# A three-part fp32 kernel: the first attention pair prepared in written order, smaller weight steps, a spread last pair, and a block diagonal copied from SBUF

## The chip, the cores and the metric

One core of a Trainium2 chip. TensorE (PE) multiplies, VectorE (DVE) and ScalarE (ACT) read its results from PSUM, GpSimd (POOL) adds from SBUF to SBUF, SyncE (SP) issues DMAs. The metric is the device time of one execution in microseconds.

## The reference, cut to what matters

```python
# q, k, v: 4 x 8 heads x 1152 x 64;  then x is 4 x 576 x 512
q_pool = q.reshape(B, H, S // 2, 2, D).mean(axis=3)
scores = scale * q_pool @ k.T;  scores -= scores.max(-1)
attn = exp(scores) / (exp(scores).sum(-1) + 1e-9);  x = attn @ v      # stage 1
# stage 2: 4 experts (two of them weighted in per token by a gate), causal attention 576 x 576
q, k, v = x @ wq[e], x @ wk[e], x @ wv[e];  out += gate * softmax(causal(q @ k.T)) @ v @ wo[e]
# stage 3: low-rank token mixing and an MLP 512 -> 2048 -> 512
u = x + (x.T @ U @ V).T;  out = u + relu(u @ w_ch1) @ w_ch2
```

U, V and the MLP's weights come as float64 and are decoded to float32 by integer operations on DVE.

## The kernel before

**Precision.** An fp32 operand of a product is cut into a high part (ACT copies it to fp32r) and a low part (DVE subtracts): `cut`, `evac_k`, `evac_q`. A score product is two matmuls with 128 contraction rows that carry high and low parts: tiles S1, S2 (from k) and Q1, Q2 (from q), held by `Pair`.

**Stage 1** works on 16 pairs of heads. A pair has 18 units (2 halves of 288 queries by 9 key blocks), and a unit has two slots (its two heads), so a pair is 36 slots. In a slot PE makes one score tile (L576, L577) and ACT its Exp (L578). After every third unit come the matmuls with v (L596). POOL adds up the denominators (L588). At the end of a half the sums, reciprocals and products follow (`post_a`, `post_r`, `post_b`; L428 to L441, L613).

**`prep(i)`** prepares pair i while pair i - 1 runs. `pool_q` adds neighbouring queries on DVE (L495). `tr_q` and `tr_k` transpose (L511, L502), ACT copies the high part (qh, kn), and one slot later DVE subtracts the low part (ql, klo). `tr_q` also sends qh by DMA into a block diagonal BD (L522). `lay` copies qh, ql, kn and klo by 12 DMAs into Q1, Q2, S1 and S2: six of 144 KB, six of 288 KB. `mxs` takes the maxima: one matmul of BD with 384 keys (L543), one reduce on DVE (L545), 27 per pair. `fin` turns the maxima of 5 or 4 query blocks by a transpose (L406), ACT copies them (`nm`, L408), and two DMAs put them as a row into Q2 (L411). L577 reads that row, so no score of a half starts before its `fin`. PSUM: `pms` has 3 buffers for maxima, transposes and sums.

**Order.** The steps stand in `side`, a list by slot; M_AT, Q_AT and the like are the slots. PE, DVE and ACT issue the loop over the slots (`attend`) in the order written (a manual region). What is emitted outside it, the whole preparation of pair 0 (all 27 maxima) and the first four steps of pair 1, and everything on SP, is ordered by the framework's planner. All DMAs are issued by SP, on one queue.

**Experts' weights** (`expert_weights`) are loaded and cut during stage 1 in six sets: wq, wk, wv with the gate, wo, U, V. A set has two 512-column cuts (wq to wo), or three decode steps of two DVE operations each and an end (U, V). The steps stand in slots 17 and 29 of a pair (WC_AT), a set every two pairs.

**Last pair.** In its slots the first expert pair is prepared: four cuts of x (XC_AT), four projections of 12 matmuls each (L684), maxima (L753) and `dmax`, which writes the maxima into Q2 on DVE (L395). `evac_q` takes a projection of q out of PSUM: two ACT copies to Q1 (L379); one slot later, for each half of the partitions, a DVE subtraction (L383), a DMA (L384) and an ACT copy of the same PSUM tile into the block diagonal (L385).

Of the kernel before, what the change touches and what calls it, by code (L numbers as in the profile page):

```python
# [27 lines left out]
WL_AT, WC_AT = 31, [17, 29]  # L28

XC_AT = [12, 13, 14, 15]  # L30
XP_AT = [18, 19, 21, 22, 25, 26, 27, 28, 29, 30, 31, 32, 33, 34, 35]
# [101 lines left out]
def kernel(  # L133
# [99 lines left out]

    def decode_steps(raw, a, b):
# [5 lines left out]
        def first():  # L240
            nc.vector.tensor_scalar(a, hi, 0x7FFFFFFF, None, op0=ALU.bitwise_and)
            nc.vector.tensor_scalar(f(a), f(a), F64_LEAST, F64_MOST, op0=ALU.max, op1=ALU.min)  # L242

        def second():
            nc.vector.tensor_scalar(a, a, 3, -0x40000000, op0=ALU.logical_shift_left, op1=ALU.bitwise_xor)  # L245
            nc.vector.tensor_scalar(b, lo, 29, None, op0=ALU.logical_shift_right)

        def third():
            nc.vector.scalar_tensor_tensor(b, a, 0x7FFFFFFF, b, op0=ALU.bitwise_and, op1=ALU.bitwise_or)
            nc.vector.scalar_tensor_tensor(b, hi, -0x80000000, b, op0=ALU.bitwise_and, op1=ALU.bitwise_or)  # L250

        return [first, second, third], f(b)

    def decode(raw, a, b):
        steps, v_ = decode_steps(raw, a, b)
        for g in steps:
            g()
        return v_

    def expert_weights():  # L260
# [16 lines left out]
        def heads(x, w, dst):  # L277
            t = part(x, NC, dst[0].shape[-1])

            def load():  # L280
                for e in range(E):
                    nc.sync.dma_start(t[:, :, e * HD:(e + 1) * HD], w[e].rearrange("(c p) d -> p c d", p=P))
                if t.shape[-1] > EW:
                    nc.sync.dma_start(t[:, :, EW:], w_gate.rearrange("(c p) e -> p c e", p=P))

            return load, pieces(t, *dst, 2)

        def out_():
            t = part(1, EP, DM)
            return (lambda: nc.sync.dma_start(t, wo.rearrange("(x e) d n -> (e d) x n", x=EP)) and None,  # L290
                    pieces(t, WO[0], WO[1], 2))
# [4 lines left out]
        def tokens_u():  # L296
            t = part(0, NTT, R, 2).bitcast(I32) if wide else part(0, NTT, R)
            steps, v_ = decode_steps(t, *(part(0, NTT, R, off=x * NTT * R).bitcast(I32) for x in (2, 3))) \
                if wide else ([], t)

            def load():
                nc.vector.memset(t[64:, full:], 0)
                m = mu.bitcast(I32) if wide else mu
                if wide:
                    nc.sync.dma_start(t[:, :full], m[:full * P].rearrange("(c p) (r w) -> p c r w", p=P, w=2))
                    nc.sync.dma_start(t[:T - full * P, full], m[full * P:].rearrange("p (r w) -> p r w", w=2))
                else:
                    nc.sync.dma_start(t[:, :full], m[:full * P].rearrange("(c p) r -> p c r", p=P))
                    nc.sync.dma_start(t[:T - full * P, full], m[full * P:])

            def end():
                cut(v_, MU[:, :, :R], MU[:, :, R:2 * R])
                nc.vector.memset(f(MU[:, :, 2 * R:3 * R]), 0.0)
                nc.scalar.activation(MU[:, :, 3 * R:], v_, AF.Copy)

            return load, steps + [end]

        def tokens_v():
# [16 lines left out]
        return [heads(0, wq, (WQK[0][:, 0], WQK[1][:, 0])), heads(1, wk, (WQK[0][:, 1], WQK[1][:, 1])),  # L335
                heads(0, wv, WVG), out_(), tokens_u(), tokens_v()]
# [39 lines left out]
    def evac_q(ps, bd, pr, sl, done):  # L376
# [36 lines left out]

    def run_all(steps):
        def run(g):
            x = g()
            for y in x if isinstance(x, tuple) else (x,):
                if callable(y):
                    run(y)

        for _, g in steps:
            run(g)
# [43 lines left out]
    def load_q(i):  # L466
        b, h0 = divmod(2 * i, H)
        qr = ld.tile([96, 2, JQ, 2, D], F32, name="qr")
        nc.sync.dma_start(qr, q[b, h0:h0 + 2].rearrange("h (p j u) d -> p h j u d", j=JQ, u=2))
        qraw[i] = qr  # L470

    def load_k(i):
# [3 lines left out]
        for j in range(0, NKT, w):  # L476
            for a in range(2):
                nc.sync.dma_start(kr[:, j:j + w, a, :],
# [3 lines left out]
    def load_v(i):  # L482
        b, h0 = divmod(2 * i, H)
        vr = per.tile([P, 2, NKT, D], F32, name="vr", bufs=2)
        nc.sync.dma_start(vr, v[b, h0:h0 + 2].rearrange("h (p j) d -> p h j d", j=NKT))
        vraw[i] = vr

    def prep(i):
# [18 lines left out]
        def tr_q(j0, j1):  # L507
# [9 lines left out]
            nc.scalar.activation(qh[:, sl], ps[:, :n], AF.Copy)  # L517

            def rest():
                nc.vector.tensor_sub(ql[:, sl], ps[:, :n], f(qh[:, sl]))  # L520
                for a in range(2):
                    nc.sync.dma_start(f(BD[i % 2][HALF[a], sl.start // 64:sl.stop // 64, HALF[a]]),  # L522
                                      f(qh[HALF[a], sl]).rearrange("p (t j) -> p t j", j=64))
# [32 lines left out]
        steps = [(POOL_AT, pool_q), (Q_AT[0], lambda: tr_q(0, 4)), (Q_AT[1], lambda: tr_q(4, JQ))]  # L556
        steps += [(at, lambda c=c: tr_k(c)) for c, at in enumerate(K_AT)]
        steps += [(LAY_AT, lay)] + [(at, lambda x=x: mxs(*x)) for at, x in zip(M_AT, order)]
        return steps + [(at, lambda x=x: fin(*x)) for at, x in zip(F_AT, BLOCKS)]
# [59 lines left out]
    P0, P1 = (sorted(prep(x), key=lambda y: y[0]) for x in range(2))  # L619
    turns = Q_AT + K_AT + [POOL_AT]  # L620
    load_q(0)
    load_k(0)
    run_all([x for x in P0 if x[0] in turns])
    load_k(1)
    load_q(1)
    load_v(0)
    run_all([x for x in P0 if x[0] not in turns and x[0] < F_AT[1]])
    run_all([x for x in P1 if x[0] < 0])
    run_all([x for x in P0 if x[0] == F_AT[1]])
    for x, (load, steps) in enumerate(expert_weights()):  # L630
        place(side, [(WL_AT, load)], n * 2 * x)
        at = [y + n * w for w in range(1, 3) for y in WC_AT]
        place(side, list(zip(at, steps)), n * 2 * x)
        assert len(steps) <= len(at)
    for i in range(NP):
        units += [unit(i, u) for u in range(2 * NKT)]
    for i in range(1, NP):
# [4 lines left out]
        place(side, [x for x in (P1 if i == 1 else prep(i)) if n0 + x[0] >= 0], n0)  # L642
# [268 lines left out]
    with tc.manual_schedule(engines={mybir.EngineType.PE, mybir.EngineType.DVE, mybir.EngineType.Activation}):  # L911
        attend(units, side)
# [186 lines left out]
```

## Time and profile before

| | |
|---|---|
| runs before, median (lowest to highest) | 1169.14 us (1166.94 to 1174.28), 3 runs |
| profiled execution: time, span | 1167.44 us, 1165.7 us |
| PE, DVE, ACT, POOL busy | 96%, 66%, 40%, 42% |
| granted TensorE clock, mean | 0.989 |
| DMA | 120.02 MB, one queue for all but instruction loads |

The span runs from the first to the last instruction; 1.7 us of the execution lie around it. Stage 1 takes the span from its start to about 500 us, stage 2 to about 760, stage 3 the rest. Matmuls are pipelined and their ends modelled, so PE's busy share hides short waits; the length of a repeated piece of work shows them.

### The profile page before, as it was taken

Reading aid. Unit: us, or ns where it says so; the run is one execution under the profiler, and the core shown is the slowest. Engines: PE = TensorE matmul, PEld = TensorE weight load, DVE = VectorE, ACT = ScalarE, POOL = GpSimd, SP = SyncE. Lnnn points to the kernel's source line nnn. Section 1 sums busy time; section 2 is a strip of 40 time slices with the busy share of each in tenths; the row PEclk is TensorE's granted clock in tenths of the full one; section 3 lists DMA queues with packets and bytes.
Section 4 is the critical chain, followed back from the end, with each engine's and each line's share of the span. In section 5 each row is a group of like instructions: output and inputs, shape, how many; then the busy total and the mean of one; then the engine's idle time right before and its main releaser. Section 6 shows DMA issues by size and latency. Waiting matters only on the chain.

```text
span 1165.7 us, 18965 instructions
## 1 busy us (share of the span) xinstructions
PE 1119.7 (96%) x6748; PEld 900.2 (77%) x6748; DVE 771.3 (66%) x1661; ACT 469.7 (40%) x1184; POOL 490.0 (42%) x382
## 2 busy tenths in 40 slices
PE   5999999999999999899999998999999999999998
PEld 3777777777777677678777775698979988999997
DVE  6687878787888877476858589989394256221222
ACT  1565656565555555544545545422221111111111
POOL 4688888888777788642212133212020011000000
PEclk7999999999999999999999999999999999999999
DMA  9787787878777664112112134363031011000111
GB/s 221 171 183 174 170 184 164 185 165 169 169 173 164 159 145 115 41 32 52 42 41 83 31 97 171 100 220 110 1 108 37 1 37 37 1 1 1 55 55 54
DMA packets 116957, 120.02 MB, mean 103 GB/s; under 512 B 71680, under 2 KB 88064, under 8 KB 116864
## 3 DMA queue, kind: packets, MB, share of 16 engines
q1 hardware_dynamic: 116864, 118.82, 41.3%
q8 instruction: 53, 0.87, 0.3%
q14 instruction: 40, 0.33, 0.1%
HBM read 52.65 MB, written 9.44 MB: 53 GB/s over the span
## 4 chain that ended last, share of the span: by engine, by line
PE 65%; DVE 17%; issue 11%; DMA 3%; ACT 2%; POOL 1%; SPq 1%; ACTq 0%; DVEq 0%; POOLq 0%
PE pv L596 10%; PE ms L1005 10%; PE o L1016 9%; PE ms L684 7%; PE st L576 7%; PE ms L543 5%; PE st L577 5%; PE pv L832 2%; DVE mp L545 2%; DVE dcb L250 1%; DVE dca L242 1%; PE ms L502 1%; DVE dca L245 1%; PE ms L603 1%; PE st L807 1%
## 5 line engine op out<-in xcount | busy, mean ns | idle before, releaser
L588 POOL TENSOR_TENSOR acc<-acc,pt 128x576 f32<-128x576 f32 x224 | 328.6, 1467 | 73.4 <-ACT pt L578 57.5
L578 ACT ACTIVATE pt<-st 128x288 f32<-128x288 f32 x576 | 218.8, 409 | 182.9 <-PE st L577 143.8
L545 DVE TENSOR_REDUCE mp<-ms 128x1 f32<-128x384 f32 x432 | 212.5, 545 | 55.0 <-PE ms L543 55.0
L1005 PE MATMUL ms<-uh,w 128*128 128x384 f32 x768 | 214.5, 340 | 0.0
L1009 DVE SCALAR_TENSOR_TENSOR hl<-ms,hh 128x384 fp32r<-128x384 f32 x96 | 53.4, 556 | 199.4 <-ACT hh L1008 199.1
L1016 PE MATMUL o<-w,hh 128*128 128x512 f32 x576 | 182.8, 397 | 1.9 <-ACT hh L1008 1.9
L543 PE MATMUL ms<-kn,bd 128*128 128x384 f32 x432 | 151.7, 361 | 13.2 <-DMA bd<-qh 7.3
L596 PE MATMUL pv<-pt,vr 128*64 128x288 f32 x1152 | 159.3, 412 | 0.0
L1008 ACT ACTIVATE hh<-ms 128x384 fp32r<-128x384 f32 x96 | 46.8, 489 | 261.8 <-PE ms L1005 261.8
L1005 PEld LDWEIGHTS ms<-uh,w 128*128 128x128 f32 x768 | 141.0, 188 | 5.0 <-issue 0.9
L232 POOL TENSOR_TENSOR w<-dcb,w 128x512 fp32r<-128x512 f32 x32 | 43.7, 1368 | 216.4 <-ACT w L231 206.8
L1005 PE MATMUL ms<-ul,w 128*128 128x384 f32 x384 | 129.6, 338 | 2.2 <-DVE ul L232 2.2
L1016 PEld LDWEIGHTS o<-w,hh 128*128 128x128 f32 x576 | 107.1, 188 | 21.0 <-ACT hh L1008 3.1
L596 PEld LDWEIGHTS pv<-pt,vr 128*64 128x64 f32 x1152 | 76.9, 136 | 54.9 <-issue 9.8
L1016 PE MATMUL o<-w,hl 128*128 128x512 f32 x288 | 114.6, 398 | 2.7 <-DVE hl L1009 2.7
L543 PEld LDWEIGHTS ms<-kn,bd 128*128 128x128 f32 x432 | 83.7, 194 | 21.4 <-DVE mp L545 12.0
L576 PE MATMUL st<-q1a,s1a 128*128 128x288 f32 x288 | 98.0, 340 | 0.7 <-ACT pt L578 0.7
L576 PEld LDWEIGHTS st<-q1a,s1a 128*128 128x128 f32 x288 | 54.2, 188 | 46.5 <-issue 40.3
L824 POOL TENSOR_TENSOR acc<-acc,pt 128x576 f32<-128x576 f32 (+4 forms) x48 | 44.2, 920 | 108.9 <-ACT pt L815 108.2
L576 PE MATMUL st<-q1b,s1b 128*128 128x288 f32 x288 | 86.2, 299 | 1.5 <-ACT pt L578 1.5
L577 PE MATMUL st<-q2a,s2a 128*128 128x288 f32 x288 | 85.4, 296 | 0.0
L577 PE MATMUL st<-q2b,s2b 128*128 128x288 f32 x288 | 85.1, 295 | 0.0
(169 smaller groups left out, 1890.2 us busy)
## 6 DMA issues: line engine op xcount, KB each, us to landing
raw<-in_moe_w_ch_dram SPq DMA_DIRECT2D x32, 512.0 KB
qr<-in_q_dram SPq DMA_DIRECT2D x16, 576.0 KB
vr<-in_v_dram SPq DMA_DIRECT2D x16, 576.0 KB
s1a<-kn SPq DMA_DIRECT2D x32, 288.0 KB
s1b<-kn SPq DMA_DIRECT2D x32, 288.0 KB
kr<-in_k_dram SPq DMA_DIRECT2D x30, 288.0 KB
s2a<-klo SPq DMA_DIRECT2D x16, 288.0 KB
s2b<-klo SPq DMA_DIRECT2D x16, 288.0 KB
```

What stands on the lines that cost most here:

```text
L543: nc.tensor.matmul(ps[:, :384], BD[i % 2][:, t, :], KN[i % 2][:, c * 384:c * 384 + 384], start=True, stop=True)
L545: nc.vector.tensor_reduce(st["mp"][:, t, c:c + 1], ps[:, :384], axis=X, op=ALU.max)
L576: nc.tensor.matmul(ps[:, :HT], pr.S1[a][:, ks], pr.Q1[a][:, qs], start=True, stop=False)
L577: nc.tensor.matmul(ps[:, :HT], pr.S2[a][:, ks], pr.Q2[a][:, qs], start=False, stop=True)
L578: nc.scalar.activation(c["pt"][:, a, :], ps[:, :HT], AF.Exp, scale=0.0625)
L588: nc.gpsimd.tensor_add(acc[i, h], acc[i, h], c["pt"])
L596: nc.tensor.matmul(o[64 * a:64 * a + 64, :HT], vr[:, a, kt, :], c["pt"][:, a, :], start=(kt == 0), stop=(kt == NKT - 1))
L684: nc.tensor.matmul(ps, stat[x][s], mov[x][m], start=(x == 0 and y == 0), stop=(x == n - 1 and y == 2))
L1005: nc.tensor.matmul(ps[:, :TB], W[fi][:, 0, a, cs], m[:, c, :], start=(c == 0 and y == 0), stop=(c == NC - 1 and y == 2))
L1008: nc.scalar.activation(h, ps[:, :TB], AF.Relu)
L1009: nc.vector.scalar_tensor_tensor(l, ps[:, :TB], 0.0, f(h), op0=ALU.max, op1=ALU.subtract)
L1016: nc.tensor.matmul(o[s_], hl[m][:, r], W[fi][:, 1, a, :], start=(fi % FG == 0 and y == 0), stop=(fi % FG == FG - 1 and y == 2))
```

## The change

1. `first_two` prepares pair 0 and begins pair 1 inside a manual region that also orders SP. v of pair 0 and q and k of pair 1 are loaded by ACT's DMA queue, issued behind ACT's copies. For pair 0 the blocks of BD are written by ACT from PSUM instead of by DMA. `lay` issues its copies of kn and qh first, those of ql and klo later. The first 15 maxima and their `fin` come before the first score; the other 12 and their `fin` go into slots 0 to 12 of pair 0 (M0_AT, F0_AT). Pair 1's maxima go into slots 13 to 37 (M1_AT), where before they took slots 3 to 37.
2. Weight steps are halved: cuts of a quarter of the set, decode steps of one operation for V (still two for U). Three slots of a pair, 17, 28 and 34, take one each, 20 slots or more after the set's load. The sets follow each other as their halves of the staging buffer come free: the steps run from pair 1 to pair 10, and wq and wk are both loaded in slot 1 of pair 0.
3. In the last pair the cuts take slots 12 to 18, the projections 20 to 27, maxima and `dmax` 28 to 35.
4. `evac_q` subtracts both halves first and then fills the block diagonal from Q1 in SBUF.

```diff
-WL_AT, WC_AT = 31, [17, 29]
-XC_AT = [12, 13, 14, 15]
-XP_AT = [18, 19, 21, 22, 25, 26, 27, 28, 29, 30, 31, 32, 33, 34, 35]
+M0_AT, F0_AT = [0, 1, 2, 3, 4, 6, 7, 7, 8, 9, 10, 10], 12
+M1_AT = [13, 13, 14, 15, 15, 16, 16, 18, 18, 19, 19, 20, 20, 21, 22, 24, 24, 25, 26, 27, 30, 30, 31, 32, 33, 36, 37]
+WC_AT, WL_AT = [17, 28, 34], 20
+XC_AT = [12, 14, 16, 18]
+XP_AT = [20, 22, 25, 27, 28, 29, 30, 31, 32, 33, 33, 34, 35, 35, 35]
...
-            return load, pieces(t, *dst, 2)
+            return load, pieces(t, *dst, 4)
...
-            return load, steps + [end]
+            return load, [lambda x=x: run_all(steps[x:x + 2]) for x in range(0, len(steps), 2)] + \
+                [lambda: cut(v_, MU[:, :, :R], MU[:, :, R:2 * R]), end]
...
                 nc.vector.tensor_sub(pr.Q1[a][HALF[1 - a], sl], ps[HALF[a]], f(pr.Q1[a][HALF[a], sl]))
                 nc.sync.dma_start(f(pr.Q2[a][HALF[a], sl]), f(pr.Q1[a][HALF[a], sl]))
+            for a in range(2):
                 nc.scalar.activation(bd[HALF[a], t0:t0 + nt, HALF[1 - a]],
-                                     ps[HALF[a]].rearrange("p (t j) -> p t j", j=64), AF.Copy)
+                                     f(pr.Q1[a][HALF[a], sl]).rearrange("p (t j) -> p t j", j=64), AF.Copy)
...
             nc.scalar.activation(qh[:, sl], ps[:, :n], AF.Copy)
+            blocks = lambda a: BD[i % 2][HALF[a], sl.start // 64:sl.stop // 64, HALF[a]]
+            if i == 0:
+                for a in range(2):
+                    nc.scalar.activation(blocks(a), ps[HALF[a], :n].rearrange("p (t j) -> p t j", j=64), AF.Copy)
...
+            kn = KN[i % 2]
+            for a in range(2):
+                for h in range(2):
+                    nc.sync.dma_start(f(pr.S1[a][HALF[h]]), f(kn[HALF[a]]))
             for a in range(2):
                 nc.sync.dma_start(f(pr.Q1[a][HALF[a]]), f(qh[HALF[a]]))
-                nc.sync.dma_start(f(pr.Q1[a][HALF[1 - a]]), f(ql[HALF[a]]))
                 nc.sync.dma_start(f(pr.Q2[a][HALF[a]]), f(qh[HALF[a]]))
-            lay_k(klo, KN[i % 2], pr, slice(0, S))
+            def low():
+                for a in range(2):
+                    nc.sync.dma_start(f(pr.Q1[a][HALF[1 - a]]), f(ql[HALF[a]]))
+                    nc.sync.dma_start(f(pr.S2[a][HALF[a]]), f(klo[HALF[a]]))
+            return low
...
+    def first_two():
+        x, y = prep(0), prep(1)
+        load_q(0)
+        load_k(0)
+        run_all([x["pool"]])
+        q0, k0, q1, k1, k2 = [g() for g in (x["q"][0], x["k"][0], x["q"][1], *x["k"][1:])]
+        for g in (load_v, load_q, load_k):
+            g(g is not load_v, nc.scalar)
+        low = x["lay"]()
+        run_all([q0, k0, q1])
+        run_all(x["m"][:5] + [k1] + x["m"][5:10] + [k2, low] + x["m"][10:15] + x["f"][:1])
+        run_all([y["pool"], *y["q"], y["k"][0]])
+        place(side, list(zip(M0_AT, x["m"][15:])) + [(F0_AT, x["f"][1])], 0)
+        place(side, list(zip(K_AT[1:], y["k"][1:])) + [(LAY_AT, y["lay"])] + list(zip(M1_AT, y["m"]))
+              + list(zip(F_AT, y["f"])), 0)
+    by_hand = {mybir.EngineType.PE, mybir.EngineType.DVE, mybir.EngineType.Activation}
+    with tc.manual_schedule(engines=by_hand | {mybir.EngineType.SP}):
+        first_two()
+    slots = [x + n * w for w in range(1, NP - 2) for x in WC_AT]
```

(`q0` to `k2` are the subtractions that follow the transposes; `pieces(..., 4)` holds for wo as well, in half rows.)

## Rows read from the trace of the kernel before

**Rows 1.** Waits of PE, whole span: who for what, us, times, longest.

```profile
PE ms L543 <- DMA bd<-qh: 7.3, 2, 6.5
PE ms L543 <- DVE mp L545: 5.7, 9, 1.7
PE ms L897 <- ACT bdb L385: 3.9, 2, 2.0
PE ms L684 <- DVE xl L232: 1.9, 2, 1.2
...
PE ms L753 <- ACT bdb L385: 0.5, 1, 0.5
```

**Rows 2.** DVE in order of time: the second maximum over blocks, one per pair.

```profile
62.19 0.17 DVE L548 TENSOR_REDUCE mx<-mp 128x4 f32<-128x12 f32 x1
...
91.15 0.17 DVE L548 TENSOR_REDUCE mx<-mp 128x4 f32<-128x12 f32 x1
...
119.20 0.17 DVE L548 TENSOR_REDUCE mx<-mp 128x4 f32<-128x12 f32 x1
...
290.38 0.17 DVE L548 TENSOR_REDUCE mx<-mp 128x4 f32<-128x12 f32 x1
...
410.54 0.17 DVE L548 TENSOR_REDUCE mx<-mp 128x4 f32<-128x12 f32 x1
```

**Rows 3.** Windows: PE, PEld, DVE, ACT, POOL busy; granted clock; DMA share; GB/s.

```profile
10.00:20.00 10.00, 3.50 (x9) 2.26 (x8) 5.88 (x12) 0.49 (x1) 5.03 (x6) 0.69 1.18 257
20.00:30.00 10.00, 9.64 (x23) 5.83 (x23) 9.51 (x22) 0.27 (x1) 0.00 (x0) 0.50 0.96 221
30.00:36.00 6.00, 4.77 (x23) 3.97 (x22) 2.36 (x7) 3.15 (x9) 1.09 (x1) 0.65 0.25 52
36.00:66.00 30.00, 30.00 (x209) 22.71 (x208) 21.36 (x44) 18.07 (x49) 25.02 (x18) 1.00 0.86 187
```

**Rows 4.** ACT and DVE in order of time, start to 35 us.

```profile
10.05 0.49 ACT L361 ACTIVATE kn<-st 128x384 fp32r<-128x384 f32 x1
...
17.20 7.54 DVE L545 TENSOR_REDUCE mp<-ms 128x1 f32<-128x384 f32 x16 [1.81 <-PE ms L543]
...
33.02 1.80 ACT L578 ACTIVATE pt<-st 128x288 f32<-128x288 f32 x4 [0.18 <-PE st L577]
```

**Rows 5.** Chain that ended last, first 60 us: start, us, what.

```profile
26.41 4.47 DMA q2a<-nm
...
37.79 0.17 PE ms L543
```

**Rows 6.** Groups of DVE, 36 to 430 us, by form: busy, mean ns, idle before.

```profile
L545 DVE TENSOR_REDUCE mp<-ms 128x1 f32<-128x384 f32 x372 | 183.2, 544 | 45.6 <-PE ms L543 45.6
...
L232 DVE TENSOR_TENSOR wqk<-stg,wqk 128x512 fp32r<-128x512 f32 x4 | 5.1, 1266 | 1.9 <-ACT wqk L231 1.9
...
L250 DVE SCALAR_TENSOR_TENSOR stg<-stg 128x576 int32<-128x576 int32 x1 | 1.9, 1858 | 0.0
...
L232 DVE TENSOR_TENSOR mu<-stg,mu 128x160 fp32r<-128x160 f32 x1 | 1.3, 1306 | 0.4 <-ACT mu L231 0.4
```

**Rows 7.** DVE in order of time, pair 1, around slot 29.

```profile
82.73 1.36 DVE L232 TENSOR_TENSOR wqk<-stg,wqk 128x512 fp32r<-128x512 f32 x1 [0.97 <-ACT wqk L231]
```

**Rows 8.** DVE, ACT and PE in order of time, stage 2, 607 to 610 us.

```profile
607.16 0.48 DVE L383 TENSOR_TENSOR q1a<-ms,q1a 64x320 fp32r<-64x320 f32 x1
...
608.14 0.49 DVE L383 TENSOR_TENSOR q1b<-ms,q1b 64x320 fp32r<-64x320 f32 x1 [0.50 <-ACT bdb L385]
...
609.15 0.75 PE L897 MATMUL ms<-ts,mv 128*128 128x512 f32 x2 [1.95 <-ACT bdb L385]
```

**Rows 9.** DVE in order of time, last pair, 470 to 500 us.

```profile
474.48 5.47 DVE L232 TENSOR_TENSOR xl<-xt,xh 128x576 fp32r<-128x576 f32 x3 [1.65 <-ACT xh L231]
...
495.95 1.54 DVE L395 TENSOR_TENSOR q2a<-negid,mx 64x320 fp32r<-64x320 f32 x1
```

**Rows 10.** PE in order of time, last pair.

```profile
492.36 0.40 PE L576 MATMUL st<-q1b,s1b 128*128 128x288 f32 x1 [1.13 <-ACT pt L578]
```

More of the change, by code (lines that the diff above doesn't have):

```diff
@@ L232, in cut, with run_all @@
         (eng or nc.vector).tensor_sub(lo, src, hi.bitcast(F32))
+    def run_all(steps):
+        for g in steps:
+            x = g()
+            for y in x if isinstance(x, tuple) else (x,):
+                if callable(y):
+                    y()
     def decode_steps(raw, a, b):
@@ L238, in decode_steps @@
         lo, hi = raw[(slice(None),) * (d + 1) + (0,)], raw[(slice(None),) * (d + 1) + (1,)]
[L240 to L252, printed above, removed]
+        nv = nc.vector
+        return [
+            lambda: nv.tensor_scalar(a, hi, 0x7FFFFFFF, None, op0=ALU.bitwise_and) and None,
+            lambda: nv.tensor_scalar(f(a), f(a), F64_LEAST, F64_MOST, op0=ALU.max, op1=ALU.min) and None,
+            lambda: nv.tensor_scalar(a, a, 3, -0x40000000, op0=ALU.logical_shift_left, op1=ALU.bitwise_xor) and None,
+            lambda: nv.tensor_scalar(b, lo, 29, None, op0=ALU.logical_shift_right) and None,
+            lambda: nv.scalar_tensor_tensor(b, a, 0x7FFFFFFF, b, op0=ALU.bitwise_and, op1=ALU.bitwise_or) and None,
+            lambda: nv.scalar_tensor_tensor(b, hi, -0x80000000, b, op0=ALU.bitwise_and, op1=ALU.bitwise_or) and None,
+        ], f(b)
     def decode(raw, a, b):
         steps, v_ = decode_steps(raw, a, b)
-        for g in steps:
-            g()
+        run_all(steps)
         return v_
@@ L290, in out_ @@
             return (lambda: nc.sync.dma_start(t, wo.rearrange("(x e) d n -> (e d) x n", x=EP)) and None,
-                    pieces(t, WO[0], WO[1], 2))
+                    pieces(t.rearrange("p x (y n) -> p (x y) n", y=2), *(w.rearrange("p x (y n) -> p (x y) n", y=2)
+                                                                         for w in WO), 4))
         wide = mu.dtype != F32
@@ L412, in put_max_row @@
                               f(nm[:n, HALF[a]]))
[L414 to L422, printed above, removed]
     def recip_a(pool, ps, w=None):
@@ L517, in tr_q @@
             nc.scalar.activation(qh[:, sl], ps[:, :n], AF.Copy)
+            blocks = lambda a: BD[i % 2][HALF[a], sl.start // 64:sl.stop // 64, HALF[a]]
+            if i == 0:
+                for a in range(2):
+                    nc.scalar.activation(blocks(a), ps[HALF[a], :n].rearrange("p (t j) -> p t j", j=64), AF.Copy)
             def rest():
                 nc.vector.tensor_sub(ql[:, sl], ps[:, :n], f(qh[:, sl]))
-                for a in range(2):
-                    nc.sync.dma_start(f(BD[i % 2][HALF[a], sl.start // 64:sl.stop // 64, HALF[a]]),
-                                      f(qh[HALF[a], sl]).rearrange("p (t j) -> p t j", j=64))
+                for a in range(2 if i else 0):
+                    nc.sync.dma_start(f(blocks(a)), f(qh[HALF[a], sl]).rearrange("p (t j) -> p t j", j=64))
                 own.update({(t, i % 2): i for t in range(sl.start // 64, sl.stop // 64)})
@@ L555, in prep @@
         order = [(t, c) for t0, t1 in BLOCKS for c in range(3) for t in range(t0, t1)]
[L556 to L559, printed above, removed]
+        return {"pool": pool_q, "q": [lambda: tr_q(0, 4), lambda: tr_q(4, JQ)],
+                "k": [lambda c=c: tr_k(c) for c in range(3)], "lay": lay,
+                "m": [lambda x=x: mxs(*x) for x in order], "f": [lambda x=x: fin(*x) for x in BLOCKS]}
     acc, pvp = {}, {}
@@ L618 @@
     n = 4 * NKT
[L619 to L634, printed above, removed]
+    def first_two():
[17 more added lines that the diff above has]
+    slots = [x + n * w for w in range(1, NP - 2) for x in WC_AT]
+    free = [0, 0]
+    for halves, load, steps in expert_weights():
+        at = max(free[h] for h in halves) + 1
+        place(side, [(at, load)], 0)
+        while slots[0] < at + WL_AT:
+            slots.pop(0)
+        for g in steps:
+            t = slots.pop(0)
+            place(side, [(t, g)], 0)
+        for h in halves:
+            free[h] = t + 1
+    assert t < (NP - NP // B) * n + 2 * NKT
     for i in range(NP):
@@ L641 @@
                 side.setdefault(max(0, n0 + at), []).append(lambda g=g, i=i: g(i))
-        place(side, [x for x in (P1 if i == 1 else prep(i)) if n0 + x[0] >= 0], n0)
+        if i > 1:
+            x = prep(i)
+            place(side, [(POOL_AT, x["pool"])] + list(zip(Q_AT, x["q"])) + list(zip(K_AT, x["k"]))
+                  + [(LAY_AT, x["lay"])] + list(zip(M_AT, x["m"])) + list(zip(F_AT, x["f"])), n0)
     bes = xes.enter_context(ExitStack())
@@ L910 @@
         place(side, list(zip(at, steps)), n * (NP - 1))
-    with tc.manual_schedule(engines={mybir.EngineType.PE, mybir.EngineType.DVE, mybir.EngineType.Activation}):
+    with tc.manual_schedule(engines=by_hand):
         attend(units, side)
```

20 lines of the change are left out of this document (10 added, 10 removed).

## The prediction

> **What bounds the kernel now.** I read the list of TensorE's waits first, then measured the length of one pair, then read the start in order of time, then the two other places that the diff touches.
>
> The waits of PE [rows 1] add up to little beside a span of 1165.7 us, and most of them stand at the places of this change: the block diagonal's DMA at the start (7.3 us), maxima waiting for DVE's reduces (5.7), a PSUM buffer that ACT's block-diagonal copy holds (3.9), the last pair's cuts (1.9). But ends of matmuls are modelled, so a wait can hide in busy time. A better measure is the time from a pair's last maximum to the next pair's [rows 2]. A pair without weight steps takes 119.20 - 91.15 = 28.05 us; the pair before it, with two cuts, 91.15 - 62.19 = 28.96. Twelve pairs, 62.19 to 410.54, take 348.35 us, where twelve clean ones would take 12 x 28.05 = 336.6. So the weight steps cost stage 1 about 11.8 us, although the list shows only half of it. Of that, the four pairs from 290.38 to 410.54, which decode U and V, lose 120.16 - 112.2 = 8.0; the cuts lose 3.8.
>
> In the stage itself PE is the bound: 30.00 us busy of 30, with DVE at 21.36 [rows 3]. At the start it is not. Until 30 us the DMA engines are full: 257 GB/s and a share of 1.18 in 10 to 20 us, 221 GB/s and 0.96 in 20 to 30, against 52 GB/s as soon as the scores begin [rows 3]. The chain of waits says the same: the row of maxima, issued at 26.41, lands 4.47 us later behind the copies of `lay` [rows 5]; then comes the first Exp, at 33.02 [rows 4]. The maxima (16 reduces from 17.20 in 7.54 us [rows 4]) run beneath these transfers.
>
> **The start.** The diff takes three things off it: 12 maxima, pair 0's block-diagonal DMA (288 KB), and SP's issue of three loads. The maxima are worth nothing there, as the transfers cover them. The block diagonal lets the maxima begin sooner, which is covered too. What decides is when the 12 copies of `lay` and the row behind them have landed. They read kn, whose last ACT copy ended at 10.05 + 0.49 = 10.54 [rows 4]; four copies to BD of at most 0.49 each now stand ahead of it, so they start at 11 to 12.5. `lay` is 6 x 144 + 6 x 288 KB = 2.65 MB; the loads on ACT's queue are 3 x 576 KB = 1.77 MB and are issued at the same time, behind the last kn copy. Before, q and v were moving while kn was still being made; now nothing that the diff orders moves between the first q and k and 11 us. Together 4.42 MB at 221 to 257 GB/s [rows 3] take 17.2 to 20.0 us, so the row lands at 29 to 32 us plus some 1 us of its own, and the first Exp, 2 us later as before, at 31 to 34. Had `lay` the engines alone, 2.65 MB would take 10.3 to 12.0 us, and the first Exp would come at about 26. I take 32.5: all that the trace shows is one full queue, which is nearer to sharing than to adding. That is 0.5 earlier than 33.02.
>
> The Trainium skill (DMA: Bandwidth & Descriptors, section "Issuing engines are not separate DMA queues") says that DMAs of SP and ACT run on the same 16 engines and interleave, and that a second issuer saves only its issuing time. By that rule the first Exp stays at 32 to 33 whatever queue the loads take; no run so far shows two queues.
>
> ACT's queue has `nm` behind the four load issues; it is needed at about 20 us, and if the ring were full it could wait until the loads drain, which ends before `lay` does. On SP the row stays last.
>
> **Pair 0.** Twelve maxima move from covered time into PE's bound stage, 12 x 0.17 [rows 5] = 2.1 us. DVE is the second cost: slots 13 to 24 now hold 17 maxima, 17 x 0.544 [rows 6] = 9.2 us, and the half's end, five more operations, at as much each 2.7 us (an estimate): 11.9 us in all, against some 10.5 us of PE (12 slots of 0.65 us without maxima, which is 28.05 less 27 x 0.17 over 36, and 17 x 0.17). I put the excess at 1.0 (0 to 2.5). The second `fin` is in slot 12 and its row is needed in slot 18, about 5 us later. Ahead of it SP's queue has the loads of wq and wk (1.05 MB, both now in slot 1), of the next q, k and v (up to 1.77 MB) and pair 1's block diagonal: 13 us at the rates above, for some 10 us of slots. I take 0.5 us for a late row. Back comes 0.8, the second wait for the block diagonal's DMA (7.3 less 6.5 [rows 1]), since pair 1's maxima start ten slots later.
>
> The clock: granted at full speed (2.4 GHz) at first, half (1.2 GHz) from within 10 to 20 us, where PE was busy for 3.50 of 10, and half through 20 to 30. It is full again in 30 to 36 from where a mean of 0.65 puts it, 34.2 us [rows 3], after PE had worked without pause on transposes and scores. Scores brought forward run at half speed until it rises, so an earlier start is worth about half of itself: 0.25 of the 0.5 goes. Sum for start and pair 0: -0.5 + 2.1 + 1.0 + 0.5 - 0.8 + 0.25 = **+2.5** (-3 to +6).
>
> **Finer weight steps.** What cost 0.9 in pair 1 was a block of DVE: 0.97 idle for ACT's copy, then 1.36 for the subtraction, in the slot of `tr_q` [rows 7]. The decode steps are two operations of up to 1.86 us each [rows 6]. A block that fits DVE's slack between two maxima costs PE nothing; 2.33 us cost 0.8 there, so the slack is about 1.5. What does half a cut cost? Half of 1266 ns is the lower end; the upper end is the whole 1266, for 160 columns took 1306 ns where 512 took 1266 [rows 6], so columns don't set the time. The Trainium skill (SBUF — State Buffer, section "Who interferes with whom") gives the reason: a DVE operation with two SBUF inputs and a GpSimd operation that reads SBUF lock each other out for the whole instruction. POOL, at 25.02 of 30 us [rows 3], is nearly always there. I take 0.95 us, and with half the wait for ACT's copy (0.45) a block of 1.4 us: under the slack at slots 17 and 28, about 0.25 over at 34, which is just ahead of `tr_q` and `tr_k`. Sixteen part cuts then cost about 2 us in place of 3.8. U keeps steps of two operations, of which those at 17 and 28 still cost about 1 each: 2.2. V's seven single ones cost 0 to 0.7 each, 2.4 together. So 6.6 in place of 11.8, **-5.2** (-8.5 to 0).
>
> **Block diagonal from SBUF.** Before, DVE's two subtractions and ACT's two copies took turns on one PSUM tile: DVE at 607.16, then, after 0.50 us idle for ACT, at 608.14; ACT's second copy ended at 609.1 and PE went on at 609.15 after 1.95 us [rows 8]. After, the tile is free when the second subtraction ends, 607.16 + 0.48 + 0.49 = 608.1: 1.0 us sooner, and this stands twice [rows 1]. What stays is DVE's being late at 607. One more wait of 0.5, of L753 [rows 1], falls the same way. **-2.4** (-4 to 0). The copy itself, SBUF for PSUM, changes an ACT that is mostly idle. In the last pair PE waited 1.13 us for an Exp queued behind the same chain [rows 10]: I count up to -1.1 there.
>
> **Last pair.** PE waits for the third and fourth cut (1.9 in all [rows 1]). These come from DVE: three subtractions in 5.47 us and a fourth after it [rows 9], and the first cut keeps slot 12. So the spread doesn't end them sooner; PE merely gets two slots (0.5 us) further meanwhile. At the end `dmax` (1.54 us and its twin [rows 9]) now stands in slot 33, with four maxima and the second `dmax` in 33 to 35: DVE is 3 us behind and PE has three buffers, about 1.1 lost. Sum with the chain of rows 10: **-0.5** (-1.6 to +2).
>
> **How the numbers follow.** +2.5 - 5.2 - 2.4 - 0.5 = -5.6, from the profiled 1167.44: 1161.8. The median of the runs is 1.7 higher; I predict 1162.5, between. Its own range is 1156 to 1168. About 1% (11.7 us) is what a measurement can tell from no change.
>
> Rivals:
> - *The queues add up* (0.18): `lay` at its own rate, first Exp at 26 to 27. Six us earlier, of which half stays lost to the half clock until 34.2: start and pair 0 come to about -0.5 to -2, and the total to 1157 to 1160. For it: the engines' share passes 1 in 10 to 20 us, so they overlap packets [rows 3]. Against: the rate stays under 260 GB/s in the ten-microsecond windows.
> - *Fine steps pay in full* (0.14): each part cut is as long as a whole one, so 11 blocks at slots 28 and 34 cost 0.4 and the decode little less than before. Gain 1.5, total 1166.
> - *The second row comes late* (0.10), slower than before: SP's order in the loop is the planner's, and if it sets pair 1's `lay` (slot 13) ahead of the row of slot 12, 2.65 MB or 11 us stand before it. It decides from where the row lands after slot 18's turn, 5 us after slot 12. Price 6 to 11, total 1168 to 1173, about 1170.
> - *The change doesn't do what it says* (0.10): the two hand-ordered regions are merged by the planner; if pair 1's `tr_k`, which waits for the second k, precedes the first score, that waits for the loads too: first Exp 34.5, total 1164.5.
>
> The forecast keeps 0.48. Range 1153 to 1171. Faster by over 1% is half of the first rival and the forecast's tail, 0.15; slower by over 1% 0.04; within 0.81.
>
> **What would show it.** First Exp between 31 and 34; DMA full from 12 to 30 us with little before; last maximum of pair 1 at 64 to 65; L548 of later pairs 28.1 to 28.8 apart; TensorE's wait for bdb gone and about 1 us for DVE's L383 in its place at 607; cuts of the last pair still ending 7 us after the first. I am wrong if the first Exp comes at 26 or before, if pairs with fine steps still take 28.9, or if PE waits in slot 18 of pair 0.

## The result, and the profile after

The changed kernel takes 1179.48 us (median of 6 runs, 1178.59 to 1181.12), the kernel before beside it 1168.04: a ratio of 1.0092, 95% interval 1.0067 to 1.0117. It is slower by about 11 us, where 5.6 us less were forecast, and outside the range. The profiled execution took 1181.12 us, 13.7 more than that of before, with a span of 1179.3.

Where the time went is read first from the marks of [rows 2], the second maximum over blocks of each pair, here in the changed kernel (DVE in order of time, one per pair):

```profile
68.61 0.17 DVE L558 TENSOR_REDUCE mx<-mp 128x4 f32<-128x12 f32 x1
...
97.49 0.17 DVE L558 TENSOR_REDUCE mx<-mp 128x4 f32<-128x12 f32 x1
...
126.32 0.17 DVE L558 TENSOR_REDUCE mx<-mp 128x4 f32<-128x12 f32 x1
...
214.09 0.17 DVE L558 TENSOR_REDUCE mx<-mp 128x4 f32<-128x12 f32 x1
...
416.78 0.17 DVE L558 TENSOR_REDUCE mx<-mp 128x4 f32<-128x12 f32 x1
```

The first mark is 6.42 us later than before: start and pair 0. That base varies: in eight traces of kernels with the start of before (its own, and those of seven of the runs below), the first Exp of pair 1 stands between 60.45 and 63.08 us; it was 61.02 before and is 67.44 now, so the start loses 4.4 to 7.0 us. From the first mark on twelve pairs take 348.17 us, against 348.35: the finer weight steps gave nothing, and a pair with three of them takes 28.88 where one without takes 28.05. Comparing the n-th Exp of the two kernels, the loss is 6.2 us at pair 13, 8.0 six Exps into stage 2, 12.5 at stage 2's end and 13.4 in stage 3. The gains that were forecast are missing, and the start costs more.

The start by windows (columns as in [rows 3]) and in order of time (SP's issues, then ACT's, then PE):

```profile
0.00:10.00 10.00, 3.25 (x16) 3.10 (x17) 4.62 (x14) 3.58 (x8) 9.15 (x20) 1.00 1.02 184
10.00:20.00 10.00, 7.23 (x16) 3.36 (x15) 8.55 (x20) 1.43 (x4) 5.04 (x6) 0.74 1.09 278
20.00:30.00 10.00, 2.10 (x9) 1.43 (x9) 0.95 (x1) 0.15 (x1) 0.00 (x0) 0.50 1.15 221
30.00:36.00 6.00, 3.44 (x12) 3.18 (x13) 2.81 (x6) 2.17 (x6) 0.00 (x0) 0.50 0.74 162
```

```profile
4.99 2.14 SPq L287 DMA_DIRECT2D stg<-in_moe_wq_dram  x4
7.17 2.38 SPq L287 DMA_DIRECT2D stg<-in_moe_wk_dram  x4
9.59 0.54 SPq L483 DMA_DIRECT2D vr<-in_v_dram  x1
...
28.90 0.84 SPq L419 DMA_DIRECT2D q2a<-nm  x1
```

```profile
33.76 0.41 ACT L587 ACTIVATE pt<-st 128x288 f32<-128x288 f32 x1 [2.82 <-PE st L586]
```

```profile
33.14 0.58 PE L586 MATMUL st<-q2a,s2a 128*128 128x288 f32 x1 [2.11 <-DMA q2b<-nm]
...
37.28 0.44 PE L586 MATMUL st<-q2b,s2b 128*128 128x288 f32 x1
...
39.83 0.29 PE L586 MATMUL st<-q2b,s2b 128*128 128x288 f32 x1
```

The DMA engines are as full as before until 30 us, and the row of maxima, made at 19.25, is issued at 28.90. PE, busy for 9.64 of the 10 us from 20 to 30 in [rows 3], is now busy for 2.10. The half clock lasts longer than before: a score takes 0.44 us up to 37.28 and 0.29 from 39.83 (1.2 and 2.4 GHz), where before full speed came at 34.2. That PE's idle time is the reason isn't shown. In the run with the last pair's projections moved (below), whose start is that of the kernel before, PE is busy for the same 9.64 us from 20 to 30, and its scores stay at half speed as long (PE in order of time):

```profile
38.91 0.44 PE L576 MATMUL st<-q1b,s1b 128*128 128x288 f32 x1
...
39.50 0.29 PE L576 MATMUL st<-q1a,s1a 128*128 128x288 f32 x1
```

PE's waits over the whole span (who for what, us, times, longest), and PE in order of time in stage 2:

```profile
PE ms L869 <- DVE mx L786: 4.4, 4, 1.3
PE ms L500 <- DMA kr<-in_k_dram: 4.1, 1, 4.1
PE ms L927 <- DVE q1b L390: 4.0, 2, 2.0
...
PE st L586 <- DMA q2b<-nm: 2.1, 1, 2.1
PE ms L553 <- DVE mp L555: 1.8, 4, 0.8
PE ms L714 <- DVE xl L235: 1.8, 2, 1.2
```

```profile
613.07 0.48 PE L927 MATMUL ms<-ts,mv 128*128 128x512 f32 x1
615.56 0.69 PE L927 MATMUL ms<-ts,mv 128*128 128x512 f32 x1 [2.01 <-DVE q1b L390]
```

The 7.3 us for the block diagonal's DMA and most of the 5.7 for the reduces [rows 1] are gone. The wait that ACT's copies ended [rows 1, 8] is as long as before, 2.0 us twice, and is ended by DVE.

### The profile page after: what moved, and what is told of

Read it like the earlier page. It is cut to its first block, busy times and chain, and to the rows that moved or that the text cites. A ratio compares the mean times of both kernels' runs of the same rounds, so it can differ in the third digit from the quotient of the medians.

```text
span 1179.3 us, 18986 instructions
## 1 busy us (share of the span) xinstructions
PE 1124.7 (95%) x6748; PEld 904.7 (77%) x6748; DVE 783.0 (66%) x1669; ACT 474.1 (40%) x1196; POOL 491.7 (42%) x382
## 3 DMA queue, kind: packets, MB, share of 16 engines
q10 hardware_dynamic: 2816, 1.77, 0.7%
## 4 chain that ended last, share of the span: by engine, by line
PE 31%; DVE 12%; issue 10%; ACT 1%; DMA 0%; POOL 0%; POOLq 0%; ACTq 0%
PE ms L1035 10%; PE o L1046 10%; PE ms L714 6%; PE pv L862 2%; DVE ms L786 1%; DVE dca L254 1%; DVE dcb L257 1%; DVE dca L253 1%; DVE dcb L256 1%; DVE dcb L255 1%; PE ms L869 1%; PE st L837 1%; DVE g_w L750 1%; DVE hl L1039 1%; DVE q2b L403 1%
```

## The experiments

Ratios are to the kernel before on the same chip, with 95% intervals. "First Exp" and "pair 0" (first Exp to that of pair 1, before 33.02 and 27.99 us) are of the profiled executions. In all of them only the part named differs from the kernel before, except the last run on the last pair.

**Each part alone.**

> Part 1 alone (pair 0 by hand, 12 maxima within its scores, loads on ACT's queue) on the kernel before; nothing is left out. Theory A, the parts add up as the two traces place them: first Exp at 33 to 34 us, pair 0 about 5.5 us longer, total 5 to 7 us above the kernel before. Rival B, the loss at the start comes only from the early loads of wq and wk that part 2 asks for: without part 2 first Exp at 29 to 31 us and a total within 2 us of before.

> Part 2 alone (part cuts and single decode steps in slots 17, 28 and 34) on the kernel before. Theory A, a part step costs as much as a whole one: pairs with three steps 28.8 us, the same total as before within 1 us. Rival B, my forecast's term: pairs with part cuts 28.1 to 28.4 us, total 3 to 6 us below before.

> Part 3 alone (last pair spread over slots 12 to 35) on the kernel before. Theory A: the maxima and the row of maxima pushed to slots 33 to 35 end in stage 2, total 1.5 to 3 us above before, with waits of TensorE for DVE's second write of maxima. Rival B, my forecast's term: between 1 us below and 1 us above.

> Part 4 alone (block diagonal filled from Q1 in SBUF) on the kernel before. Theory A: the two waits of 2 us in stage 2 stay, as DVE's order decides them; total within 1 us of before. Rival B, my forecast's term: the waits shrink to 1 us, total 2.4 to 3.5 us below before.

Measured: start 1.0055 (1.0028 to 1.0082), first Exp 34.03, pair 0 32.49; weights 1.0001 (0.9980 to 1.0022); last pair 1.0043 (1.0026 to 1.0060); block diagonal 1.0016 (0.9995 to 1.0036). Their sum, 1.15%, agrees within the intervals with the 0.92% of all four. So two parts cost, two do nothing that can be measured, and none gains. The first two went as theory A has them, and so did the waits of the fourth; the last pair costs more than either theory.

**The start.** First the loads that came ahead of `lay` were held back:

```
             g(g is not load_v, nc.scalar)
         low = x["lay"]()
...
+        load_v(1)
+        for load, _ in sets[:2]:
+            load()          # wq, wk: on SP, behind the rows
```

> Part 1 alone, with the loads of wq, wk and the next v held behind the row of maxima on SP (issued inside the hand-ordered region), so that the planner can't set them ahead of lay. Theory A, those 1.6 MB ahead of lay delayed the first Exp: it comes at 28 to 30 us instead of 34, total 0 to 2 us above before. Rival B, the first Exp hangs on the loads of ACT's queue: it stays at 33 to 34, total 5 to 6 us above.

1.0059 (1.0040 to 1.0078); first Exp 33.24, pair 0 34.37. Theory A fell: the hoisted loads cost about 0.8 us (33.24 for 34.03), which is less than the first Exp varies where the start is unchanged (32.02 to 33.02 in the eight traces), and the whole is no shorter. They moved while kn was still being made: from 0 to 10 us the DMA engines move 183 GB/s with them and 118 without. SP issued the row 1.7 us sooner, at 27.31, and it landed 5.3 us later; PE had waited 5.9 for pair 1's k.

Then all 27 maxima went back ahead of the first score (without and with the loads held back), with pair 1's in the slots of the kernel before:

```
-        run_all(x["m"][:5] + [k1] + x["m"][5:10] + [k2, low] + x["m"][10:15] + x["f"][:1])
+        run_all(x["m"][:5] + [k1] + x["m"][5:10] + [k2, low] + x["m"][10:15] + x["f"][:1]
+                + x["m"][15:] + x["f"][1:])
```

> Part 1 alone, but all 27 maxima and both rows of pair 0 before its first score, and pair 1's maxima in their old slots 3 to 37. Theory A, the maxima within the scores cost what covered maxima don't: first Exp as in part 1 alone (34 us), from there to pair 1's first Exp 28 to 28.5 us instead of 32.5, total 1 to 2 us above before. Rival B, pair 0 is long because TensorE's clock is still half when its scores begin: 31 us or more, total 4 to 6 us above.

> Both of these together: loads held back and all maxima ahead of the scores. Theory A, two separate causes: first Exp at 28 to 30 us, pair 0 28 to 30 us, total 2 to 5 us below before. Rival B, they cover each other (the maxima become the path once the transfers are short): first Exp at 32 or later, total within 1 us of before.

The first: 1.0013 (0.9993 to 1.0033), first Exp 33.44, pair 0 30.12, pair 1 begins 2.5 us later than before and not 5.5. So the twelve maxima in the scores, with pair 1's crowded behind them, cost 3 us; the total is theory A's, pair 0 lies between the theories, and the scores run at half clock until 38 us here too (0.45 at 37.82). The second: 1.0058 (1.0040 to 1.0076), first Exp 34.68, pair 0 34.4. It doesn't separate anything: the order that was built sets the first score, waiting 5.9 us for `lay`, ahead of the last two maxima.

What does the first Exp hang on? All three loads were moved to SP behind the rows, and with them pair 1's transposes had to go into slots 3 to 11 and its maxima back into the later slots:

```
-        for g in (load_v, load_q, load_k):
-            g(g is not load_v, nc.scalar)
         low = x["lay"]()
...      # all maxima and both rows
+        for g in (load_v, load_q, load_k):
+            g(g is not load_v)
```

> Part 1's start with two of its choices undone at once: the loads of v of pair 0 and of q and k of pair 1 stay on SP and follow the rows, so that nothing but the rows moves up to the first score, and all 27 maxima stand before that score, with pair 1's transpositions in slots 3 to 11. Theory A (the first Exp hangs on the bytes that must move before it): with some 0.9 MB fewer ahead of the row of maxima that row lands by 28 to 30 us, the first Exp starts at 28.5 to 30.5 where it started at 33.02 to 34.7 so far, pair 0 takes 30 us as with all maxima first, and pair 1 starts 0.5 to 2.5 us before that of the kernel before: ratio 0.998 to 1.000. Rival B (the row has a price of its own after the maxima, whatever else moves): first Exp at 32 or later, pair 1 starts 1.5 to 3 us later, ratio 1.001 to 1.003.

1.0097 (1.0075 to 1.0119), a ratio that neither theory has, but the first Exp comes at 26.12, sooner than even theory A (ACT in order of time, then PE's waits up to 66 us):

```profile
26.12 2.82 ACT L589 ACTIVATE pt<-st 128x288 f32<-128x288 f32 x6 [0.15 <-PE st L588]
```

```profile
PE ms L511 <- DVE qp L495: 12.9, 2, 6.5
PE ms L555 <- DMA bd<-qh: 4.5, 1, 4.5
```

With 1.77 MB fewer beside `lay`, the first Exp comes 7 us sooner than in either kernel, and pair 0 takes 45.6: pair 1's q, queued on SP behind the second row, holds PE 6.4 us in pair 0, and its block diagonal, queued behind the loads, 4.5. The bytes move in any case; what was not carried ahead of the first score is waited for within pair 0. Two more runs moved along that line: pair 1's q ahead of the row, then pair 1's block diagonal by ScalarE's copies as well.

> The start with all 27 maxima first and the rows on SP ahead of other loads, as in the run with loads behind the rows, but q of pair 1 is issued ahead of the row of maxima, and v of pair 0, k of pair 1 and the weights behind it. Theory A (the bytes ahead of the first score set it, and pair 0 was long there only because q of pair 1 came at 33.9 us): first Exp at 28 to 30 us, pair 0 in 30 to 33, pair 1 starts 0 to 3 us before that of the kernel before, ratio 0.998 to 1.000. Rival B (pair 0 then waits for k of pair 1 and for the blocks of its diagonal, queued behind 2 MB of loads): pair 0 in 35 or more, pair 1 starts 3 us late or more, ratio 1.003 or more.

> The start with the next pair's q brought forward, and the block diagonal of pair 1 copied by ScalarE from PSUM as for pair 0, so that it doesn't queue behind 2.3 MB of loads. Theory A (that DMA, 5.7 us of waiting, was what made pair 0 long there): first Exp at 27.5 to 28.5 us, pair 0 in 32 to 36, pair 1 starts between 1 us before and 3 us after that of the kernel before, ratio 1.000 to 1.004. Rival B (k of pair 1 or the maxima crowded into fewer slots take its place): pair 0 in 38 or more, ratio 1.006 or more.

The first: 1.0075 (1.0047 to 1.0103), first Exp 27.98, pair 0 41.2, PE waiting 5.7 us for the diagonal (theory B). The second: 1.0025 (1.0010 to 1.0041), first Exp 27.93, pair 0 35.1, as theory A says: the diagonal's DMA was 6 us of pair 0. Pair 1 still begins 2.0 us later than before, at 63.05, which is no later than the latest of the eight traces. None of the seven starts beat the one there was.

**Weight steps.** Coarse steps in the changed slots:

```
-            return load, pieces(t, *dst, 4)
+            return load, pieces(t, *dst, 2)
```

> Part 2 alone, but with whole cuts and two-operation decode steps in the new slots 17, 28 and 34 (16 blocks instead of 28). Theory A, a block in slot 28 or 34 has its price whatever its size: pairs with three whole cuts 28.7 to 29.0 us, half as many of them as with part cuts, total 1.5 to 3 us below before. Rival B, the price goes by DVE's time: pairs with three whole cuts 29.5 us or more, total as before within 1 us.

1.0013 (0.9994 to 1.0033); a pair with three whole cuts takes 29.5 us, as rival B has it, with three halves 28.8, but there are twice as many halves, and the totals can't be told apart: slots 28 and 34 have no slack for either. The same half cut in its three slots, in the changed kernel (DVE in order of time):

```profile
80.84 0.90 DVE L235 TENSOR_TENSOR wqk<-stg,wqk 128x256 fp32r<-128x256 f32 x1
...
88.52 1.61 DVE L235 TENSOR_TENSOR wqk<-stg,wqk 128x256 fp32r<-128x256 f32 x1 [0.46 <-ACT wqk L234]
...
94.44 1.36 DVE L235 TENSOR_TENSOR wqk<-stg,wqk 128x256 fp32r<-128x256 f32 x1
```

The slot sets most of the time, not the columns: whole cuts, in the run with coarse steps, take 1.17, 1.66 and 1.62. Taking the stretch from one Exp to the next as a slot, DVE in a clean pair of the kernel before is idle 1.74 us in slot 5, 0.67 in 17, 1.52 in 29, 0.79 in 35, about half a microsecond in 11 and 23, and hardly elsewhere. So:

```
-WC_AT, WL_AT = [17, 28, 34], 20
+WC_AT, WL_AT = [5, 17, 29], 20
```

> Part 2 alone with its steps in slots 5, 17 and 29 in place of 17, 28 and 34. In a pair without steps VectorE stands idle 1.74 us in slot 5, 0.67 in slot 17 and 1.52 in slot 29, and not at all in 18 to 20, 28, 30 to 34 and 0 to 4. Theory A (a step is free where VectorE is idle and costs its time where it is not): stage 1's price for the weights falls from 11.8 us to 2 to 6, ratio 0.995 to 0.998. Rival B (a step costs its time in any slot, because ScalarE's half or the PSUM tiles queue behind it): the price stays at 9 to 12 us, ratio 0.999 to 1.001.

0.9964 (0.9947 to 0.9981): theory A by the ratio; over twelve pairs the price is 9.1 us, of which 3.9 fell in pair 1 (below). A half cut in slot 5 or 17 adds nothing, one in 29 mostly 0.5 us; U's steps of two operations still cost, 1.2 us in one pair. DVE, then POOL, around slot 5 of that kernel:

```profile
124.47 0.65 DVE L232 TENSOR_TENSOR wqk<-stg,wqk 128x256 fp32r<-128x256 f32 x1 [0.43 <-ACT wqk L231]
```

```profile
123.43 1.41 POOL L589 TENSOR_TENSOR acc<-pt 128x576 f32<-128x576 f32 x1 [0.65 <-ACT pt L582]
124.92 1.48 POOL L592 TENSOR_TENSOR acc<-acc,pt 128x576 f32<-128x576 f32 x1
```

The cut ends at 125.12, 0.28 us after POOL's accumulation that ran when it began (123.43 + 1.41). It is so with all 43 half cuts of three kernels up to 215 us: each ends 0.28 to 0.31 us after an accumulation does, whether it took 0.42 us or 1.65; all eight whole cuts of the run with coarse steps end 0.55 or 0.56 us after one. No run moved POOL's work, so this is read from the traces alone. In this run pair 1 lost 3.9 us (2.7 of them a wait for a block diagonal's DMA); its weights were loaded ahead of the first rows. Loads from slot 31 on, and then fewer steps in slot 29:

```
-        at = max(free[h] for h in halves) + 1
+        at = max(31, 60 * halves[-1], max(free[h] for h in halves) + 1)
```

```
-    slots = [x + n * w for w in range(1, NP - 2) for x in WC_AT]
+    slots = [x + n * w for w in range(1, NP - 2) for x in WC_AT
+             if x < 29 or w in (2, 4, 6, 7, 8, 9)]
```

> As the run with weight steps in slots 5, 17 and 29, but the weights are loaded from slot 31 of pair 0 on, as in the kernel before, and the first step stands in slot 17 of pair 1. Theory A (that run lost 4.0 us in pair 1, where the loads put the blocks of a diagonal late, and 0.5 us in each slot 29 with a step): stage 1's price for the weights falls to 4 to 6 us of the 11.8, ratio 0.993 to 0.996. Rival B (the loss in pair 1 only moves to where the loads now fall): as that run, ratio 0.996 to 0.998.

> The same, with slot 29 used in six pairs alone and slots 5 and 17 in all. Theory A (a cut is free in slots 5 and 17 and costs 0.5 us in slot 29): 1 to 3 us shorter than the run before it in this call, ratio 0.991 to 0.995. Rival B (the work costs somewhere in each pair, whichever slot): equal to it within 1 us.

0.9966 (0.9950 to 0.9982) and 0.9952 (0.9936 to 0.9968), 1165.02 us: the second is the shortest kernel of the study, though not told apart from the first. The first's ratio is rival B's and its price theory A's; by the medians the second is 1.2 us shorter, as its theory A has it, but the intervals overlap. Marks of the second, pairs 1 to 4 and 13 (DVE in order of time):

```profile
63.42 0.17 DVE L552 TENSOR_REDUCE mx<-mp 128x4 f32<-128x12 f32 x1
...
91.53 0.17 DVE L552 TENSOR_REDUCE mx<-mp 128x4 f32<-128x12 f32 x1
...
120.38 0.17 DVE L552 TENSOR_REDUCE mx<-mp 128x4 f32<-128x12 f32 x1
...
148.47 0.17 DVE L552 TENSOR_REDUCE mx<-mp 128x4 f32<-128x12 f32 x1
...
404.76 0.17 DVE L552 TENSOR_REDUCE mx<-mp 128x4 f32<-128x12 f32 x1
```

Pair 3, with two half cuts in slots 5 and 17, takes 28.09 us, a clean one 28.05. Over twelve pairs the price is 341.34 less 336.6, 4.7 us, where it was 11.8; with slot 29 in every pair (the run before) it is 6.0.

**The last pair.** Its projections and maxima alone, cuts as before:

```
-XP_AT = [18, 19, 21, 22, 25, 26, 27, 28, 29, 30, 31, 32, 33, 34, 35]
+XP_AT = [20, 22, 25, 27, 28, 29, 30, 31, 32, 33, 33, 34, 35, 35, 35]
```

> The kernel before with the new slots of the last pair's projections and maxima alone (two in slot 33, three in 35); the cuts keep slots 12 to 15. Part 3 as a whole cost 0.43 per cent. Theory A (the crowd of evacuations and reductions at slots 33 to 35 makes VectorE late at the change of stage, and PE waits there): nearly all of it is here, +3.5 to +6.5 us at the first Exps of stage 2, ratio 1.003 to 1.006. Rival B (the later cuts make the projections late): +0 to +1.5 us, ratio 0.999 to 1.001.

1.0040 (1.0023 to 1.0057): theory A, nearly all of it is here. PE's waits from 480 to 540 us, and DVE in order of time:

```profile
PE ms L603 <- DVE mx L756: 2.1, 1, 2.1
...
PE st L808 <- DVE q2b L395: 1.0, 1, 1.0
```

```profile
502.64 0.49 DVE L395 TENSOR_TENSOR q2a<-negid,mx 64x320 fp32r<-64x320 f32 x1
503.16 1.58 DVE L395 TENSOR_TENSOR q2b<-negid,mx 64x320 fp32r<-64x320 f32 x1
```

`dmax` starts at 502.64 where it started at 495.95 [rows 9], and the kernel is 5.0 us behind at stage 2's seventh Exp. Of these, 1.2 stood already at the first Exp of the last pair and come from the start, which is unchanged; the last pair lost 3.7. The same part undone in the changed kernel:

> The changed kernel with the last pair's cuts, projections and maxima back in the slots of the kernel before. Theory A (the crowd at slots 33 to 35 costs in the changed kernel what it costs alone, 0.40 to 0.43 per cent): 4 to 5 us shorter than the changed kernel, ratio to the kernel before 1.004 to 1.007. Rival B (in the changed kernel other waits take its place at the change of stage): within 2 us of the changed kernel, ratio 1.008 to 1.011.

1.0076 (1.0049 to 1.0103), with a ratio between the theories: 1.4 us under the changed kernel by the medians, as rival B has it, and the intervals overlap. The traces say the same: from the last pair's first Exp to stage 2's seventh the changed kernel loses 1.8 us against before, and none with the part undone. So among the others this part costs less than alone; what takes its place wasn't sought.

**The block diagonal.** In stage 2 the planner orders PE, and reading from SBUF changed that order (L927 stands twice in a row in the lines of stage 2 above, with no score between). Both sources were therefore run with PE in the order of the source there:

```
-    stream(units, side)
+    with tc.manual_schedule(engines={mybir.EngineType.PE}):
+        stream(units, side)
```

> The kernel before with stage 2's instructions on PE kept in the order of the source, for comparison with the next kernel alone. Both theories: the wait for the experts' block diagonal in PSUM stays near 2 us at both places; the time as a whole may differ from before by up to 1 per cent either way, as the order of stage 2 is another.

> The same with the block diagonal read from SBUF, so that PE's order is that of the kernel before it here. Theory A (ScalarE's copies only hid behind the subtraction on VectorE that reads the same PSUM tile, which ends about as late): the wait at both places changes by less than 0.4 us and is now put down to VectorE; the time is within 0.1 per cent of that kernel's. Rival B (the gain was there and the planner's new order ate it): the wait falls to about 1 us twice, and the kernel is 2 to 3 us shorter than its partner.

1.0614 (1.0585 to 1.0643) and 1.0603 (1.0567 to 1.0640): 1.0 us apart by the medians, less than the runs can tell. Both stand further from the kernel before than the 1 per cent expected, and the wait from PSUM is 2.9 and not 2. The wait, whole span, first from PSUM, then from SBUF:

```profile
PE ms L897 <- ACT bdb L385: 5.8, 2, 2.9
```

```profile
PE ms L898 <- DVE q1b L383: 4.0, 2, 2.0
```

The source takes 0.9 us off each of these waits and DVE's subtraction is next, between the theories' figures. Under the planner even that doesn't show. DVE and ACT before, then DVE and PE with that part alone:

```profile
603.00 4.13 DVE L720 COPY g_w<-g_g 32x10 f32<-32x10 f32 x16
...
608.68 0.42 ACT L385 ACTIVATE bdb<-ms 64x320 fp32r<-64x320 f32 x1
```

```profile
603.44 4.13 DVE L721 COPY g_w<-g_g 32x10 f32<-32x10 f32 x16
607.58 0.48 DVE L383 TENSOR_TENSOR q1a<-ms,q1a 64x320 fp32r<-64x320 f32 x1
608.08 0.49 DVE L383 TENSOR_TENSOR q1b<-ms,q1b 64x320 fp32r<-64x320 f32 x1
...
608.72 0.77 PE L898 MATMUL ms<-ts,mv 128*128 128x512 f32 x1 [2.02 <-DVE q1b L383]
609.28 0.44 PE L808 MATMUL st<-q1b,s1b 128*128 128x288 f32 x1
```

What makes DVE late both times is 16 copies of the gate's weights, 4.13 us. Behind them the tile is free after 1.0 us where it took 1.97 before (607.13 to 609.10). But PE waited 2.02 for 1.95: in the planner's new order a score and two matmuls with v that stood ahead of the wait now stand behind it.

## Why the prediction was wrong, step by step

By the Exps, the 13.6 us between the two spans are: start and pair 0 +6.4 (forecast +2.5), weight steps -0.2 (-5.2), last pair +1.8 (-0.5), stage 2 +4.6 (-2.4), stage 3 +1.0.

- *What bounds the kernel* held: full DMA engines up to the first score, PE in the stage, 11.8 us for the weight steps.
- *First Exp* (32.5): 33.76, on the transfers as argued, though the terms given there add up to 31 to 35.5 and not to 31 to 34. The step that failed is "nothing that the diff orders moves between the first q and k and 11 us": SP, freed, took wq, wk and the second v from 4.99 to 10, and these went ahead of `lay`, at some 0.8 us. The Trainium skill (DMA: Bandwidth & Descriptors, section "Issuing engines are not separate DMA queues") has two issuers share the same engines. The trace agrees: 278 and 221 GB/s with two queues, 257 and 221 with one [rows 3], and with 1.77 MB beside `lay` the first Exp came at about 33 on either queue, without them at 26.12. The rival that queues add up is out.
- *Pair 0* (+3.05: 2.1 + 1.0 + 0.5 - 0.8 + 0.25): +5.7, against a base of 27.99 that is the shortest of the eight traces (27.99 to 31.06), so that some of it is the base's luck. The mis-sized terms are the clock and DVE's excess. Slots 0 to 4 take 0.80 us each where the later ones with one maximum take 0.44 to 0.48; with the first matmuls with v that is some 2 us, where I had 0.25. I had counted only scores brought forward, and not that the half clock could last until 38 us; why it did stays open, as it does so in traces with the old start and the same PE work too. Slots 15, 16, 19 and 20 take 0.87 to 1.00 where they took 0.37 to 0.50, and slot 23 takes 3.29 for 2.24 as `fin` waits for the reduces: 3 us for the maxima there, of which 1.2 is PE's own work on seven more of them (in the 2.1) and some 2 DVE's excess, where I had 1.0. The late row (0.5) never came; that rival is out.
- *The rival that the loads' k precedes the first score* was right on the order (PE waits 4.1 us for k) and wrong on the price: `lay` ends later still.
- *Finer weight steps* (-5.2): -0.2 here, 1.2 less in twelve pairs alone. By the marks pairs 1 to 5, with nearly all of the cuts, lose 5.2 us (145.48 less 5 x 28.05; forecast 2, before 3.8), and the decode steps 6.3 (forecast 4.6, before 8.0). Two steps failed: the half cut at 0.95 us, whatever the slot (it took 0.90, 1.61 and 1.36), and the slack of 1.5, read off slot 29 and assumed for 28 and 34. This is the rival of paying in full.
- *Block diagonal* (-2.4): nothing measured, 1.0016. The tile was free 1.0 us sooner, as forecast; the step that failed is that PE would come to the wait with the same work done. Part of the 4.6 us that stage 2 lost in the changed kernel's trace goes with two stretches at half clock, behind the two waits (615 to 620 us: 0.66). This part of the change isn't needed for them: the run of the start alone, with the block diagonal from PSUM, has them behind the same waits and loses 1.6 and 1.3 us there. The rest stays open.
- *Last pair* (-0.5): +5.0 alone by the runs, +1.8 in the changed kernel's trace. I saw the crowd at slots 33 to 35 and priced it at 1.1; alone it was 3.1 us of new waits and a half clock behind them (0.97 over 469 to 520 us), while the 1.1 us of [rows 10] did go.

## What to carry to other kernels

Before moving hidden work, price it where it lands, on every engine: these maxima cost nothing under the transfers and 3 us within the scores. Look for an off-path engine's slack slot by slot, not per pair: the same steps, moved from slots 28 and 34 to slots 5 and 29, turned no gain into 0.36 to 0.48%. Where a planner orders an engine or a queue, a freed place is filled by something else, so compare the built order before pricing the edit. And before reading a loss of a few microseconds from two traces, ask how far the unchanged stretch varies: here the same start gave pair 1 a place anywhere in 2.6 us.

## What the runs showed of the hardware

- A cut's own work is short: 0.28 us for 256 columns, 0.55 for 512. The rest of its time on DVE is waiting for the end of POOL's accumulation, 1.4 us long: 0.42 us in all where that was about to end, 0.65 in slot 5, 0.90 in 17, 1.3 in 29, 1.4 in 34, 1.6 in 28. The Trainium skill (SBUF — State Buffer, section "Who interferes with whom") describes the lock: a DVE operation with two SBUF inputs and a GpSimd operation that reads SBUF exclude each other, for the whole instruction. The traces agree, with 42 of 43 ends at 0.28 to 0.29 us.
- The granted clock of a window can miss a slow stretch: the run with the loads held back shows 1.00 from 30 to 36 us while its scores take 0.45 us each. The length of a known matmul is the surer sign.
- Stretches at half clock follow some of PE's waits of 1 to 2 us and not others, where code and wait are the same: behind the wait of 1.95 us at 609 us [rows 8] the kernel before keeps full speed, and the run of the start alone, after 1.95 us there too, falls to half. Runs of the kernel before alone range from 1166 to 1176 us.
